# Attention decode with a squared-ReLU layer: the input is loaded twice, some matmuls change places, and two weight loads become one

## The chip, the cores and the metric

The kernel runs on one core of a Trainium2 chip. The metric is device time in microseconds (us) of one execution; the time of a kernel is the median of its runs.

## The reference, cut to what matters

Two tokens (B = 2) of width D = 512 go through one attention block with a long cache and one dense block, each after a layer norm and each with a residual:

```python
B, Sq, D = 2, 1, 512;  H, Sk, Dh = 32, 8192, 128;  F = 1792      # float32
q = (layernorm(x) @ wq) per head
p = softmax(q . k_cache * Dh ** -0.5)          # 64 pairs of head and token, 8192 keys each
h = x + (p . v_cache, heads side by side) @ wo
r = relu(layernorm(h) @ w1 + b1)
out = h + (r * r) @ w2 + b2
```

Each of the 64 pairs of head and token has 4 MB of keys and 4 MB of values, and each is read once. Nearly all of the 561 MB that the kernel reads is this cache.

## The kernel before, in words

**Storage.** One large SBUF tile, `ring`, has three places of 64 KB in each of 128 partitions. A place holds the keys and values of one pair. Place 2 first holds `wq` and, at the end, `wo`; place 0 holds `w1` and `w2` at the end.

**Beginning (lines 205 to 311).** The SP queue, which issues every load, issues `wq` into place 2, then the 2 rows of `x` into `xr` (line 210), then pairs 0 and 1 (line 212). A load is spread over 16 DMA engines, and each of them works off its share in the order in which it was issued; the 128 rows of 64 KB make eight packets for each engine. When `x` is there, DVE and ACT compute the layer norm of its two rows into `xnr` (lines 263 to 268). TensorE turns `xnr` into `xn` and `xr` into `hT` with four matmuls each against `ident`, multiplies `xn` with `wq` and turns the result into `QT`. When the last matmul that reads `wq` is over, SP issues pair 2 into place 2 (line 302).

**Loop (lines 321 to 365).** For 60 pairs, TensorE computes scores into one half of PSUM, DVE takes their maximum, ACT the exponentials, and DVE multiplies them with the values and adds up (four `scalar_tensor_tensor` of 2048 columns). SP issues the next pair into a place as soon as it is free.

**End (lines 470 to 598).** The last four pairs are written out one by one. `GROUPS` joins the partial results of the four quarters of the cache: group 0 has the heads 0 to 30, group 1 the last head. `wo` comes in as its first half, early, and then in pieces of 8, 6 and 2 heads (`WO_PIECES`); `w1` comes in three pieces and `w2` in five (`W2_PIECES`, blocks of 256 KB). `project` multiplies finished heads with `wo` into the PSUM bank `hp`. The last head's part goes another way: its effect on the normed input comes through `woc`, and its effect on the sum is added to the output bank `o`. `hidden` is the first dense layer (into `y`, bank 2 of `S[0]`). `y` is turned by DVE into `yT`; `a1` and `a2` are the bias and the squared ReLU. The second layer adds 14 blocks of four matmuls of 128 columns into `o`, which is copied to `res` and stored.

**Order and waits.** Outside the loop, instructions are recorded in a list (`Line.op`) in the written order, and `Line.plan` (line 68) finds the waits. Each tile's columns that an instruction reads or writes are remembered, with who wrote or read them; the rows (partitions) of a tile are not part of what is remembered:

```python
        return ap.tensor.name, lo, hi
```

An instruction waits for what touched the same columns before, if one of the two is a write, unless the same engine did it:

```python
                            if source == engine and (engine == "pe" or not w):
                                continue
                            needs[source] = max(needs.get(source, 0), n)
```

A load that SP issues is remembered as a source of its own, `("load", number)`, and not as `"sp"`. A wait stands in front of the waiting instruction in its engine's queue, and what is queued behind it waits as well. In addition, a load waits until the load eight before it has landed (`AHEAD`). The loads of pairs 0 to 2 in the beginning, lines 212 and 302, are given to SP by hand and carry no memory of what they write, save that line 302 waits for what reads place 2.

Of the kernel before, what the change touches and what calls it, by code (L numbers as in the profile page):

```python
# [4 lines left out]
AF = mybir.ActivationFunctionType  # L5
ALU = mybir.AluOpType
# [3 lines left out]
B, H, SK, DH, D, F = 2, 32, 8192, 128, 512, 1792  # L10
P = 128
NQ = 4
CS = SK // NQ
NH = DH // 32
DB = D // P
FB = F // P
FQ = F // NQ
BH = H * B
# [4 lines left out]
BLK = 512  # L23
GROUPS = [(0, 31), (31, 32)]
W1_PIECES = [2, 1, 1]
WO_PIECES = [8, 6, 2]
BIAS = 32
W2_PIECES = [4, 4, 3, 2, 1]
AHEAD = 8
# [141 lines left out]
def attention_block_kernel(nc, xd, kvd, wqd, wod, w1d, w2d, out):  # L171
    def sb(name, *shape):
        return nc.alloc_sbuf_tensor(name, [P, *shape], F32).ap()

    written = nc.alloc_semaphore("written")
    line = Line(nc)
# [8 lines left out]
    def place(u):  # L185
        return ring[:, u * ROW : (u + 1) * ROW]
# [11 lines left out]
    WO = place(2).rearrange("p (h c) -> p h c", h=H)  # L198
    b1T = ring[:, SLOTS * ROW : SLOTS * ROW + FB]
    b2T = ring[:, SLOTS * ROW + FB : SLOTS * ROW + FB + DB]  # L200
    W1 = place(0)[:, : DB * F].rearrange("p (d c) -> p d c", d=DB)
# [1 line left out]


    xr = sb("xr", D)
    xnr = sb("xnr", D)
    line.load(place(2), wqd)
    line.memset(xr, 0.0)
    line.memset(xnr, 0.0)
    line.load(xr[:B], xd)  # L210
    for i in range(2):
        line.op("sp", lambda e, i=i: e.dma_start(slot(i), kvd[i]).then_inc(kv_full[i], 16))
    line.op("sp", lambda e: e.sem_inc(s_free, 2))
# [4 lines left out]
    eps_t = sb("eps_t", 1)  # L218
# [3 lines left out]
    ident = sb("ident", P)  # L222
# [3 lines left out]
    quads = ident.rearrange("p (j m) -> p j m", j=NQ)  # L226
# [3 lines left out]
    def banks(k):  # L230
        return [S[k][:, n * BLK : (n + 1) * BLK] for n in range(NQ)]

    def clear(ap, n):
        line.act(ap, zero.to_broadcast([P, n]), AF.Copy)

    part = sb("part", B)
    xc = sb("xc", DB, B)
# [18 lines left out]
    bk = banks(1)  # L256
    clear(bk[0], BLK)
    clear(bk[1], BLK)
    xn = sb("xn", DB, B)
    hT = sb("hT", DB, B)  # L260
    xs = sb("xs", D)
    sx = sb("sx", 2)
    line.reduce(sx[:B, :1], xr[:B], ALU.add)
    line.fused(xnr[:B], sx[:B, :1].to_broadcast([B, D]), -1.0 / D, xr[:B], ALU.mult, ALU.add)
    line.fused(xs[:B], xnr[:B], 1.0, xnr[:B], ALU.mult, ALU.mult, accum_out=sx[:B, 1:])
    line.act(sx[:B, 1:], sx[:B, 1:], AF.Sqrt, bias=eps_t[:B], scale=1.0 / D)
    line.reciprocal(sx[:B, 1:], sx[:B, 1:])
    line.times(xnr[:B], xnr[:B], sx[:B, 1:])
    for t, (to, row) in enumerate(((xn, xnr), (hT, xr))):
        cols = bk[3][:, t * DB * B : (t + 1) * DB * B].rearrange("p (d b) -> p d b", b=B)  # L270
        for d in range(DB):
            line.matmul(cols[:, d, :], row[:, d * P : (d + 1) * P], ident[:, :B])
        line.copy(to, cols)
    warm = sb("warm", 1)
    line.act(warm, eps_t, AF.Exp)
    fold = sb("fold", 32)
# [3 lines left out]
    pick_all = sb("pick_all", P)  # L280
# [3 lines left out]
    for k in range(2):  # L284
        for d in range(DB):
            for j in range(NQ):
                n = k * NQ + j
                line.matmul(bk[k][32 * j : 32 * j + B, :], xn[:, d, :], WQ[:, d, n * BLK : (n + 1) * BLK],
                            start=(d == 0), stop=(d == DB - 1))
        line.act(big[:, k * BLK : (k + 1) * BLK], bk[k], AF.Copy)  # L290
    turned = bk[2][:, :BH].rearrange("p (k j m b) -> p k m j b", k=2, j=NQ, b=B)
    for k in range(2):
        for m in range(NQ):
            at = k * BLK + m * DH
# [11 lines left out]
    NM, LS, AC = ALL[:, :, 0], ALL[:, :, 1], ALL[:, :, 2:]  # L306
    OT = sb("OT", BH)
# [22 lines left out]
    with nc.Fori(0, LOOPED, SLOTS, engines=[ENGINE.PE, ENGINE.DVE, ENGINE.Activation],  # L330
                 head_slot={ENGINE.PE: 0, ENGINE.DVE: 128, ENGINE.Activation: 128}) as i0:
        for u in range(SLOTS):
            k = u % 2
            s, bk = S[k], banks(k)
# [6 lines left out]
            for n in range(CS // BLK):  # L341
                for j in range(NQ):
                    made = pe.matmul(bk[n][32 * j : 32 * j + 32, :], q3[:, u, :], keys(u)[:, j, n * BLK : (n + 1) * BLK],  # L343
                                     start=True, stop=True)
# [13 lines left out]
            for e in range(NH):  # L358
                v = values(u)[:, e]
                made = dve.scalar_tensor_tensor(v, v, 1.0, s, op0=ALU.mult, op1=ALU.mult,  # L360
                                                accum_out=st3[:, u, 2 + e : 3 + e])
# [12 lines left out]
    def maximum(i, k):  # L374
        line.reduce(NM[:, i : i + 1], S[k], ALU.max, negate=True)

    def exponentials(i, k):
        line.act(S[k], S[k], AF.Exp, bias=NM[:, i : i + 1], accum_out=LS[:, i : i + 1])

    def weighted(i, k, e, lo, hi, acc, by=1.0):  # L380

        v = values(i)[:, e, lo:hi]
        line.fused(v, v, by, S[k][:, lo:hi], ALU.mult, ALU.mult, accum_out=acc)

    def back(i, k, e):
        weighted(i, k, e, 0, CS, AC[:, i, e : e + 1])

    gm, w, lw, rl = (sb(n, BH) for n in ("gm", "w", "lw", "rl"))
# [6 lines left out]
    def weigh_max(n, pn):  # L395

        a, b = g_at[n]
        pn = pn[:, : NQ * (b - a)].rearrange("p (j i) -> p j i", j=NQ)
        for j in range(NQ):
            line.matmul(pn[:, j], pick[:, j, :], NM[:, a:b])  # L400

    def weigh_exp(n, pn):

        a, b = g_at[n]
        nb = b - a
        line.reduce(gm[:, :nb], pn[:, : NQ * nb].rearrange("p (j i) -> p i j", j=NQ), ALU.min)
        line.tensor(w[:, :nb], gm[:, :nb], NM[:, a:b], ALU.subtract)

    def weigh_rest(n, pl):

        a, b = g_at[n]
        nb = b - a
        line.tensor(lw[:, :nb], LS[:, a:b], w[:, :nb], ALU.mult)
        line.matmul(pl[:, :nb], pick_all, lw[:, :nb])
# [17 lines left out]
    def project(hs, hp):  # L432

        for h in hs:
            j = h % NQ
            line.matmul(hp[32 * j : 32 * j + B, :], OT[:, h * B : (h + 1) * B], WO[:, h, :],
                        start=(h < NQ), stop=(H - 1 - h <= NQ))

    def turn_rows(hp, ph):
        line.act(rows, hp, AF.Copy)  # L440
        ph = ph[:, : DB * B].rearrange("p (d b) -> p d b", b=B)
        for d in range(DB):
            line.matmul(ph[:, d, :], rows[:, d * P : (d + 1) * P], fold[:, :B])
        return ph
# [9 lines left out]
    def load_wo(a, b):  # L454

        cut = slice(a * D, b * D + (BIAS if b == H else 0))
        line.load(ring[:, 2 * ROW :][:, cut], wod[:, cut])
# [9 lines left out]
    bk0, bk1 = banks(0), banks(1)  # L467
# [29 lines left out]
    at = H // 2  # L497
    for n in WO_PIECES:
        load_wo(at, at + n)
# [14 lines left out]
    at = 0  # L514
# [3 lines left out]
    at = 0  # L518
# [4 lines left out]
    hp, sums, y, o = bk0  # L523
    y, o = y[:, :FQ], o[:, :P]
    clear(hp, D)
    clear(y, FQ)
    clear(o, P)
    maximum(last, 1)
    exponentials(last, 1)
    a, b = g_at[1]  # L530
    weigh_max(1, sums[:, :64])
    project(range(H // 2), hp)
    weigh_exp(1, sums[:, :64])
    line.act(w[:, :B], w[:, :B], AF.Exp)
    back(last, 1, 0)
    weigh_rest(1, sums[:, 64:128])
    line.act(warm, w[:, 0:1], AF.Sqrt)
    back(last, 1, 1)
    back(last, 1, 2)
    line.reciprocal(rl[:, :B], sums[:, 64 : 64 + B])  # L540
# [7 lines left out]

    line.times(aw2[:, 0, :NH], AC[:, last - 1, :], w[:, 0:1])
    line.times(aw2[:, 1, : NH - 1], AC[:, last, : NH - 1], w[:, 1:2])  # L550
    project(range(H // 2, H - 1), hp)
    ph = turn_rows(hp, sums[:, 192:256])
    weighted(last, 1, NH - 1, 0, CS // 2, aw2[:, 1, NH - 1 : NH], by=w[:, 1:2])
    weighted(last, 1, NH - 1, CS // 2, CS, aw2[:, 1, NH : NH + 1], by=w[:, 1:2])
# [2 lines left out]
    for e in range(NH + 1):  # L557
        at = 32 * min(e, NH - 1)
# [12 lines left out]
    def hidden(ds):  # L571
        for d in ds:
            for j in range(NQ):
                line.matmul(y[32 * j : 32 * j + B, :], xc[:, d, :], W1[:, d, j * FQ : (j + 1) * FQ],
                            start=(d == 0), stop=(d == DB - 1))
# [3 lines left out]
    line.matmul(var, ones_d, squares(xc))  # L579
    scale_of(var)  # L580
    hidden(range(2, DB))
    for j in range(NQ):
        line.matmul(o[32 * j : 32 * j + B, :], hT[:, j, :], ident, start=True, stop=False)
        line.matmul(o[32 * j : 32 * j + B, :], OT[:, a:b], WO[:, H - 1, j * P : (j + 1) * P], start=False, stop=False)
    yT = sb("yT", FB, 32)
    line.turn(yT.rearrange("p m r -> p (m r)"), y)
    a1 = sb("a1", FB, B)
# [4 lines left out]
    for m in range(FB):  # L592
        for j in range(NQ):
            line.matmul(o[32 * j : 32 * j + B, :], a2[:, m, :], W2[:, m, j * P : (j + 1) * P],
                        start=False, stop=(m == FB - 1))
    res = sb("res", P)
    line.copy(res, o)
    line.op("sp", lambda e: e.dma_start(out, res).then_inc(written, 16), [res], [])
# [35 lines left out]
```

## Time and profile before

| | us |
|---|---|
| median of 3 runs | 1303.70 |
| lowest and highest | 1303.56, 1303.97 |
| the profiled execution, whole | 1303.94 |
| its span, first to last instruction | 1302.6 |
| busy: DVE | 742.5 (57%) |
| busy: TensorE | 399.9 (31%) |
| busy: ACT | 143.9 (11%) |
| busy: DMA engines (16 together) | 99.7% of the span |
| read from HBM | 561.01 MB, 431 GB/s |

The 1.34 us between the span and the whole time lie before the first and after the last recorded instruction. PE is the TensorE matmul, DVE the VectorE, ACT the ScalarE, and SPq the queue of SyncE, which issues the transfers. A DMA's time to landing runs from its issue until its semaphore is complete.

### The profile page before, as it was taken

What the parts mean: (1) busy time and instruction counts of PE and PEld (TensorE: products, weight loads), DVE (VectorE), ACT (ScalarE), POOL (GpSimd) and SP (SyncE); (2) the same over time, 40 slices, a digit from 0 to 9 for tenths busy, and PEclk for the clock granted to TensorE, in tenths of its full rate; (3) what the DMA queues carried; (4) which work ended last, traced back from release to release, by engine and by line L of the source; (5) the groups of instructions that cost most, each with busy time, mean ns of one, the idle gap of its engine ahead of it and who ended that gap; (6) DMA issues with size and microseconds to landing.
All of it is one profiled execution on the core that took longest, in us unless ns stands there. A gap on an engine that the chain in (4) does not pass through costs nothing. (4 is left out here: it accounts for less than half of the span.)

```text
span 1302.6 us, 6694 instructions
## 1 busy us (share of the span) xinstructions
PE 399.9 (31%) x2424; PEld 109.8 (8%) x2424; DVE 742.5 (57%) x705; ACT 143.9 (11%) x149; POOL 0.7 (0%) x6
## 2 busy tenths in 40 slices
PE   1523223223313313322322322322322331331437
PEld 1100000000000000000000000000000000000113
DVE  1355665665665564665565565566566566557464
ACT  1011010011011011011011011101101101101111
POOL 0000000000000000000000000000000000000000
PEclk9676666667667667667667667666766756666657
DMA  9999999999999999999999999999999999999998
GB/s 419 420 445 425 443 427 441 427 439 431 433 437 421 447 423 445 425 445 425 443 425 439 431 435 435 425 443 423 445 425 445 425 443 425 441 429 437 420 429 363
DMA packets 11820, 561.19 MB, mean 431 GB/s; under 512 B 1314, under 2 KB 1442, under 8 KB 2468
## 3 DMA queue, kind: packets, MB, share of 16 engines
q1 hardware_dynamic: 11812, 561.08, 99.7%
q8 instruction: 5, 0.08, 0.0%
q14 instruction: 3, 0.02, 0.0%
HBM read 561.01 MB, written 0.07 MB: 431 GB/s over the span
## 5 line engine op out<-in xcount | busy, mean ns | idle before, releaser
L360 DVE SCALAR_TENSOR_TENSOR ring<-ring,s 128x2048 f32<-128x2048 f32 x240 | 534.7, 2283 | 136.2 <-DVEq L314 136.2
L343 PE MATMUL s<-ring,q 128*32 128x512 f32 x1920 | 333.0, 857 | 816.3 <-PEq L314 816.3
L349 DVE TENSOR_REDUCE st<-s 128x1 f32<-128x2048 f32 x60 | 137.5, 2292 | 325.3 <-DVEq L314 325.3
L355 ACT ACTIVATE s<-s,st 128x2048 f32<-128x2048 f32 x60 | 116.5, 1942 | 1031.7 <-ACTq L314 1031.7
L343 PEld LDWEIGHTS s<-ring,q 128*32 128x32 f32 x1920 | 84.5, 151 | 1064.0 <-issue 1064.0
L158 DVE SCALAR_TENSOR_TENSOR ring<-ring,s 128x2048 f32<-128x2048 f32 x15 | 33.6, 2283 | 6.6 <-ACT s L140 6.6
L136 PE MATMUL s<-ring,QR 128*32 128x512 f32 x128 | 24.3, 930 | 38.5 <-DMA ring<-in_kvd 24.9
L162 DVE TENSOR_REDUCE ALL<-s 128x1 f32<-128x2048 f32 x4 | 9.2, 2290 | 21.3 <-PE s L136 21.3
L360 DVE DVE_READ_ACCUMULATOR ring<-ring,s 128x1 f32 x240 | 19.8, 82 | 0.0
L364 DVE TENSOR_SCALAR ALL<-st 128x6 f32 x60 | 10.3, 171 | 15.1 <-DVEq L314 15.1
L140 ACT ACTIVATE s<-s,ALL 128x2048 f32<-128x2048 f32 x4 | 7.8, 1942 | 51.7 <-DVE ALL L162 51.7
L162 DVE TENSOR_REDUCE sx<-xr 2x1 f32<-2x512 f32 x1 | 0.7, 674 | 20.6 <-DMA xr<-in_xd 20.6
L355 ACT ACTIVATION_READ_ACCUMULATOR s<-s,st 128x1 f32 x60 | 11.6, 193 | 0.0
L136 PEld LDWEIGHTS s<-ring,QR 128*32 128x32 f32 x128 | 5.4, 162 | 56.3 <-DMA ring<-in_kvd 26.8
L136 PE MATMUL s<-ring,OT 128*2 128x512 f32 (+1 forms) x70 | 10.0, 701 | 0.0
L136 PE MATMUL s<-ident,xnr 128*128 128x2 f32 x8 | 1.9, 355 | 25.9 <-DVE xnr L154 25.9
L136 PE MATMUL s<-ring,xn 128*2 128x512 f32 x64 | 9.7, 773 | 0.0
L154 DVE TENSOR_SCALAR QT<-s 128x64 f32<-128x64 f32 x1 | 0.2, 224 | 10.6 <-PE s L136 10.6
L136 PE MATMUL s<-ring,a 128*2 128x128 f32 x112 | 4.8, 327 | 3.3 <-DMA ring<-in_w2d 2.2
L140 ACT ACT_TABLE_LOAD x4 | 5.1, 1283 | 0.8 <-PEq L627 0.7
L136 PE MATMUL s<-ALL,pick 128*128 128x62 f32 (+1 forms) x16 | 3.6, 369 | 4.8 <-DVE ALL L162 4.8
L351 DVE TENSOR_SCALAR q<-QT 128x96 f32 x20 | 4.9, 243 | 0.0
(84 smaller groups left out, 58.1 us busy)
## 6 DMA issues: line engine op xcount, KB each, us to landing
ring<-in_kvd SPq DMA_DIRECT2D x3, 4096.0 KB, 32.0
ring<-in_wod SPq DMA_DIRECT2D x1, 4096.0 KB, 28.6
ring<-in_kvd SPq DMA_DIRECT2D x1, 3072.0 KB, 28.1
ring<-in_wod SPq DMA_DIRECT2D x1, 2048.0 KB, 32.7
ring<-in_w2d SPq DMA_DIRECT2D x2, 1024.0 KB, 18.0
ring<-in_w1d SPq DMA_DIRECT2D x1, 1792.0 KB, 33.7
ring<-in_w1d SPq DMA_DIRECT2D x2, 896.0 KB, 23.6
ring<-in_wod SPq DMA_DIRECT2D x1, 1536.0 KB, 35.9
```

The lines of the kernel that those rows point to most:

```text
L136: self.op("pe", lambda e: e.matmul(out, lhsT, rhs, start=start, stop=stop), [lhsT, rhs], [out])
L140: self.op("act", lambda e: e.activation(out, in_, func, bias=bias, scale=scale, accum_out=accum_out), [in_, *more], [out] + ([] if accum_o ...
L154: self.op("dve", lambda e: e.tensor_scalar(out, in_, by, None, op0=ALU.mult), [in_, *more], [out])
L158: self.op("dve", lambda e: e.scalar_tensor_tensor(out, a, by, b, op0=op0, op1=op1, accum_out=accum_out), [a, b, *more], [out] + ([] if acc ...
L162: self.op("dve", lambda e: e.tensor_reduce(out, in_, axis=AX.X, op=op, negate=negate), [in_], [out])
L343: made = pe.matmul(bk[n][32 * j : 32 * j + 32, :], q3[:, u, :], keys(u)[:, j, n * BLK : (n + 1) * BLK], start=True, stop=True)
L349: dve.tensor_reduce(nm, s, axis=AX.X, op=ALU.max, negate=True).then_inc(m_full, 1)
L351: dve.tensor_scalar(q3, QT[:, bass.ds(i0 + SLOTS, SLOTS), None].to_broadcast([P, SLOTS, 32]), 1.0, None, op0=ALU.mult)
L355: act.activation(s, s, AF.Exp, bias=nm, scale=1.0, accum_out=ls).then_inc(e_full, 1)
L360: made = dve.scalar_tensor_tensor(v, v, 1.0, s, op0=ALU.mult, op1=ALU.mult, accum_out=st3[:, u, 2 + e : 3 + e])
L364: dve.tensor_scalar(ALL[:, bass.ds(i0 + u, 1)], st3[:, u : u + 1], 1.0, None, op0=ALU.mult).then_inc(kv_free, 1)
```

## The change

- `x` is loaded twice, by two loads in a row, into rows 0 to 1 and rows 32 to 33 of `xr`. The tile `xnr` and its clearing are dropped; the layer norm works in place on rows 32 to 33. One matmul per block of 128 columns now turns both pairs of rows, so four turns take the place of eight, with `hT` copied first and `xn` second.
- `WO_PIECES` is `[10, 6]` in place of `[8, 6, 2]`: one load fewer.
- Of the first 16 heads, seven are projected before the last pair's maximum is used, while DVE takes it, and nine after it. Of the other 15, the ten of the first piece come ahead of the matmul that sums the last head's `lw`, and five come later.
- The eight small matmuls that add `hT` and the last head to `o` move from ahead of the turn of `y` to behind the first four blocks of the second layer. In their old place stands one matmul of 512 columns whose result nobody reads.

```diff
-WO_PIECES = [8, 6, 2]
+WO_PIECES = [10, 6]
+EARLY = 7
...
-    xnr = sb("xnr", D)
     line.load(place(2), wqd)
     line.memset(xr, 0.0)
-    line.memset(xnr, 0.0)
-    line.load(xr[:B], xd)
+    for at in (0, 32):
+        line.load(xr[at : at + B], xd)
     for i in range(2):
         line.op("sp", lambda e, i=i: e.dma_start(slot(i), kvd[i]).then_inc(kv_full[i], 16))
...
+    xs = sb("xs", D)[32 : 32 + B]
+    sx = sb("sx", 2)[32 : 32 + B]
+    xnr = xr[32 : 32 + B]
...
-    for t, (to, row) in enumerate(((xn, xnr), (hT, xr))):
-        cols = bk[3][:, t * DB * B : (t + 1) * DB * B].rearrange("p (d b) -> p d b", b=B)
-        for d in range(DB):
-            line.matmul(cols[:, d, :], row[:, d * P : (d + 1) * P], ident[:, :B])
-        line.copy(to, cols)
+    cols = bk[3][:, : 2 * DB * B].rearrange("p (d t b) -> p d t b", t=2, b=B)
+    for d in range(DB):
+        line.matmul(cols[:, d], xr[:, d * P : (d + 1) * P], quads[:, :2, :B])
+    line.copy(hT, cols[:, :, 0])
+    line.copy(xn, cols[:, :, 1])
...
+    project(range(EARLY), hp)
     maximum(last, 1)
     exponentials(last, 1)
     a, b = g_at[1]
     weigh_max(1, sums[:, :64])
-    project(range(H // 2), hp)
+    project(range(EARLY, H // 2), hp)
...
-    weigh_rest(1, sums[:, 64:128])
+    line.tensor(lw[:, :B], LS[:, a:b], w[:, :B], ALU.mult)
     line.act(warm, w[:, 0:1], AF.Sqrt)
+    project(range(H // 2, H // 2 + WO_PIECES[0]), hp)
+    line.matmul(sums[:, 64 : 64 + B], pick_all, lw[:, :B])
...
-    project(range(H // 2, H - 1), hp)
+    project(range(H // 2 + WO_PIECES[0], H - 1), hp)
...
-    for j in range(NQ):
-        line.matmul(o[32 * j : 32 * j + B, :], hT[:, j, :], ident, start=True, stop=False)
-        line.matmul(o[32 * j : 32 * j + B, :], OT[:, a:b], WO[:, H - 1, j * P : (j + 1) * P], start=False, stop=False)
+    line.matmul(bk1[0][:B], xc[:, 0, :], W1[:, 0, :BLK])
...
-                        start=False, stop=(m == FB - 1))
+                        start=(m == 0), stop=(m == FB - 1))
+        if m == W2_PIECES[0] - 1:
+            for j in range(NQ):
+                at = o[32 * j : 32 * j + B, :]
+                line.matmul(at, hT[:, j, :], ident, start=False, stop=False)
+                line.matmul(at, OT[:, BH - B :], WO[:, H - 1, j * P : (j + 1) * P], start=False, stop=False)
```

More of the change, by code (lines that the diff above doesn't have):

```diff
@@ L260, in attention_block_kernel @@
     hT = sb("hT", DB, B)
[L261 to L268, printed above, removed]
-    for t, (to, row) in enumerate(((xn, xnr), (hT, xr))):
-        cols = bk[3][:, t * DB * B : (t + 1) * DB * B].rearrange("p (d b) -> p d b", b=B)
-        for d in range(DB):
-            line.matmul(cols[:, d, :], row[:, d * P : (d + 1) * P], ident[:, :B])
-        line.copy(to, cols)
+    xs = sb("xs", D)[32 : 32 + B]
+    sx = sb("sx", 2)[32 : 32 + B]
+    xnr = xr[32 : 32 + B]
+    line.reduce(sx[:, :1], xnr, ALU.add)
+    line.fused(xnr, sx[:, :1].to_broadcast([B, D]), -1.0 / D, xnr, ALU.mult, ALU.add)
+    line.fused(xs, xnr, 1.0, xnr, ALU.mult, ALU.mult, accum_out=sx[:, 1:])
+    line.act(sx[:, 1:], sx[:, 1:], AF.Sqrt, bias=eps_t[32 : 32 + B], scale=1.0 / D)
+    line.reciprocal(sx[:, 1:], sx[:, 1:])
+    line.times(xnr, xnr, sx[:, 1:])
+    cols = bk[3][:, : 2 * DB * B].rearrange("p (d t b) -> p d t b", t=2, b=B)
[3 more added lines that the diff above has]
+    line.copy(xn, cols[:, :, 1])
     warm = sb("warm", 1)
```

## The prediction

> **What bounds the kernel now.** I read the page first: its queue table says whether any engine matters at all.
>
> ```profile
> span 1302.6 us, 6694 instructions
> ...
> q1 hardware_dynamic: 11812, 561.08, 99.7%
> ```
>
> The one queue of loads keeps the 16 DMA engines busy for 99.7% of the span. So the kernel takes as long as 561 MB take, plus what lies before the first packet and after the last. An edit counts if it makes the engines stand idle, or if it shortens the two ends. The chain that ended last shows the back end:
>
> ```profile
> 1279.92 17.98 DMA ring<-in_w2d
> 1297.90 0.04 issue
> 1297.95 2.74 PE s L136 x48
> 1300.69 0.02 issue
> 1300.71 0.29 DVE res L147
> ```
>
> The last matmuls run 2.74 us without a pause, then comes the copy and the store. The front end is in the timeline (start, duration, engine, operation):
>
> ```profile
> 0.75 0.39 SPq L133 DMA_DIRECT2D ring<-in_wqd  x1
> 1.43 0.32 SPq L133 DMA_DIRECT2D xr<-in_xd  x1
> 1.80 0.94 SPq L212 DMA_DIRECT2D ring<-in_kvd  x2
> ...
> 22.66 0.67 DVE L162 TENSOR_REDUCE sx<-xr 2x1 f32<-2x512 f32 x1 [20.56 <-DMA xr<-in_xd]
> ```
>
> `x` is only 4 KB, but it lies behind the 8.4 MB of `wq` and lands at about 22.64. Pairs 0 and 1 are issued at 1.80, long before that. The table of stretches shows what this early issue buys (last column GB/s of the packets that start in the stretch, before it the summed packet time as a share of 16 engines):
>
> ```profile
> 1.50:1.75 0.25, 0.00 (x0) 0.00 (x0) 0.25 (x1) 0.25 (x1) 0.00 (x0) 1.00 0.00 0
> 1.75:2.00 0.25, 0.00 (x0) 0.00 (x0) 0.25 (x2) 0.25 (x1) 0.00 (x0) 1.00 8.76 2884
> 2.00:2.25 0.25, 0.00 (x0) 0.00 (x0) 0.10 (x3) 0.14 (x2) 0.00 (x0) 1.00 3.96 1311
> ...
> 21.50:21.75 0.25, 0.00 (x0) 0.00 (x0) 0.00 (x0) 0.00 (x0) 0.00 (x0) 1.00 1.21 524
> 21.75:22.00 0.25, 0.00 (x0) 0.00 (x0) 0.00 (x0) 0.00 (x0) 0.00 (x0) 1.00 2.45 1057
> 22.00:22.25 0.25, 0.00 (x0) 0.00 (x0) 0.00 (x0) 0.00 (x0) 0.00 (x0) 1.00 4.88 2105
> 22.25:22.50 0.25, 0.00 (x0) 0.00 (x0) 0.00 (x0) 0.00 (x0) 0.00 (x0) 1.00 1.21 524
> 24.00:25.00 1.00, 0.00 (x0) 0.00 (x0) 0.74 (x3) 0.19 (x1) 0.00 (x0) 1.00 2.42 1049
> ```
>
> A packet is 64 KB, so GB/s times the width counts packets. Eleven engines start their first packet between 1.75 and 2.00, five by 2.25. Those 16 packets take 8.76 x 0.25 + 3.96 x 0.25 = 3.18 us each. In the round at 24 they take 2.42. Between 21.5 and 22.5 the engines pass, one after the other (2, 4, 8, 2), from `wq` straight to pair 0, at 22.03 in the mean.
>
> **The second load of `x`: the one edit that touches the stream.** Both loads write the same columns of `xr`, in other rows. The planner remembers columns only, and a load is a source of its own, so the second load waits on SP until the first has landed. Behind it in SP's queue are pairs 0 and 1. They are now issued after `wq` has been read to the end, and all 16 engines run dry. The working:
> - The first load lands as before: 22.64. SP needs some 0.06 to go on (the second piece of `w1` is issued at 1262.71 behind a landing at 1262.65), so the second load of `x` is issued at 22.70. Pair 0 follows 0.37 later (1.43 to 1.80 before), at 23.07.
> - From issue to packets: `wq` was issued at 0.75 and its packets start at 1.95 in the mean (the middles of the two stretches, 11 and 5 engines): 1.20. So pair 0 starts at 24.27 in place of 22.03: **+2.24**. It can't be a gain, as there is nothing else to read. At its lowest the delay is 1.9: the store of the result has its first packets 0.84 after its issue.
> - The first packets into idle engines took 3.18, later ones 2.42. If pair 0 starts as `wq` did, that adds **+0.76**. The bounds are 0 (only the start of the execution is slow) and 0.76; I take 0.76, since this is the same kind of load, into as many idle engines, and no nearer row exists.
>
> The Trainium skill ("DMA: Bandwidth & Descriptors", Anatomy of one DMA) speaks against this edit too: a DMA has some 2 us of fixed cost, mostly the receipt of its last write, which only overlap hides. By that figure alone the price would be 2.0 in place of 3.0. The rows say more, since they hold the slower first packets as well.
>
> Nothing gives the delay back, as the loop is bound by the stream: pair 3 is issued at 64.56, when pair 2 is still coming in until some 82.
>
> **The rest of the beginning: nothing.** The second load lands at about 24.2 (the store, as small, took 1.5 from issue to landing), 1.55 later than `x` before. Four turns fewer give 1.87 back (eight instructions fewer at 27.98 for 1.87), and one clearing of 0.48 on DVE was never waited for. So the queries are ready at about 41.9 as before. Pair 2 is issued at 39.54, some 20 us before pair 1 is in: that is its cover, and pair 2 is due no earlier than before.
>
> **One load of `wo` fewer.** The bytes and their order stay. Between 1204 and 1297, with 18 smaller loads, the stretch moves 424 GB/s; the loop from 100 to 1200 moves 433. That is 2.1% of 93 us, 1.9 us in all and at most 0.11 for one load; part of it is instruction fetches. I take **-0.05**, between 0 and -0.11. Loads are issued as early as before or earlier, with 17 us and more from issue to landing, so none comes late.
>
> **Projections.** Seven heads go into 2.42 us in which TensorE waited for the last maximum. Two rounds of four, two passes each, take about 0.43 a pass at full clock: 1.7. At half clock they would push the joining by 1 us. Ten heads must now end before `lw` is summed: they may start when their piece lands, about 1276.1, and take 20 x 0.12 to 0.19 us, to 1279 or so; the sum was wanted at 1279.94. Five heads remain behind the last piece (1279.86) where fifteen ran until 1282.66, so `hT` comes some 0.8 earlier. None of it shows in the end: `hidden` waits for the last piece of `w1` at 1291.04. Without this cover, 0.8 would be a gain, and a late join a loss of up to 1. Price 0.
>
> **The matmuls in the second layer.** The eight small ones (1291.91 to 1292.54, 0.63 busy) lay beside the turn of `y` and cost nothing there. In their new place they fill the wait for the second piece of `w2`: the first four blocks end at 1294.72, plus 0.63 is 1295.35, and the piece lands at 1296.02. The unread matmul, two passes of 512 columns at 0.43 or 0.85 each, runs from 1292.1 to 1293.0 or 1293.8; the second layer begins at 1293.64. Cost 0, at most 0.2. What they can change is the clock. In these stretches of 3.41 us the second number is TensorE's busy time, and the third from the end its granted clock:
>
> ```profile
> 1267.45:1270.86 3.41, 1.18 (x12) 0.12 (x4) 2.15 (x1) 0.00 (x0) 0.00 (x0) 0.99 0.95 406
> 1270.86:1274.27 3.41, 3.22 (x16) 2.04 (x20) 1.42 (x4) 2.96 (x4) 0.00 (x0) 0.50 1.01 429
> ...
> 1291.34:1294.75 3.41, 2.25 (x56) 1.19 (x48) 1.31 (x4) 0.00 (x0) 0.00 (x0) 1.00 1.02 423
> 1294.75:1298.17 3.42, 1.28 (x40) 0.96 (x44) 0.00 (x0) 0.00 (x0) 0.00 (x0) 0.99 0.94 376
> 1298.17:1301.58 3.41, 2.47 (x48) 1.16 (x37) 0.29 (x1) 0.00 (x0) 0.00 (x0) 0.50 0.10 34
> ```
>
> After 1.18 and 1.28 busy the next stretch has half clock, after 2.25 full clock. The moved matmuls make the second to last one 1.28 + 0.63 = 1.91, nearer to 2.25. At full clock an instruction takes 1.05/32 = 0.033 us, at half 2.74/48 = 0.057. The last piece of `w2` lands at 1299.8, and its eight instructions then end at about 1300.1 in place of 1300.69: -0.55 at best. The Trainium skill ("TensorE: Matmul & The Clock Gate", Part 1) says that the window of 3.4 us runs freely, so that its position differs from run to run; one profile can't show that here. I take **-0.45**, between 0 and -0.55.
>
> **Sum.** From the profiled execution: 1303.94 + 2.24 + 0.76 - 0.05 - 0.45 = **1306.4**, which is 2.7 above the median of 1303.70 (the profiled execution was 0.24 above it). 0.2% of the time, about what a measurement of this kernel can tell from no change, is 2.6 us, up to 1306.3; the forecast lies just beyond it.
>
> **Rivals.**
> - *The engines restart at full pace* (not slower by 0.2%). Place: the first round of pair 0. Price: the 0.76 falls away, 1305.7; with first packets 0.84 after the issue 1305.3. It decides as soon as first packets take under about 3.05. For it: the slow packets are seen only at the very start of the execution. Against it: nothing in the profile shows idle engines that start a load quickly. Chance 0.31. The Trainium skill's fixed 2 us, named above, belongs to this rival (1303.94 + 2.0 - 0.05 - 0.45 = 1305.4).
> - *The end runs at half clock.* The moved matmuls then end at 1293.67 + 48 x 0.057 = 1296.4, past the landing at 1296.02, and the remaining 80 instructions end 4.57 later, at 1301.0, 0.3 later than before: 1303.94 + 2.95 + 0.3 = 1307.2. Against it: TensorE has more work than before in the windows that decide. Chance 0.08.
> - *The change doesn't do what I read*: pairs 0 and 1 get out before `x` lands, or are hidden. Then only the end moves: 1303.94 - 0.5 = 1303.4. The order of SP's queue speaks against it. Chance 0.04.
>
> **How the numbers follow.** The forecast has 0.57, of which 0.50 is over 0.2% slower and 0.07 (the end fully gained) is not; its own range is 1306.0 to 1306.9. The restart adds 0.02 to slower and 0.29 to the same, the half clock 0.08 to slower, the last rival 0.03 to the same and 0.01 to faster. Together: slower 0.60, same 0.39, faster 0.01. The range reaches from the restart rival (1305.1) to the half clock (1307.3).
>
> **What would show it.** Right: SP issues the second `x` at 22.7 and pair 0 at 23.1; no 64 KB packet starts between 22.5 and 24.0; the first round then lasts about 3.2; the loop is the same, 3 us later. Wrong: pair 0 issued before 22, a first round of 2.4 us, or a last piece of `w2` that lands at other than 1302.1 to 1303.

## The result and the profile after

The changed kernel takes 1306.27 us (median of 17 runs, 1305.88 to 1307.4), the kernel before 1303.82 (17 runs, 1303.51 to 1304.9): 2.45 us or 0.19% slower, ratio 1.002 with the 95% interval [1.0012, 1.0027]. The forecast was 1306.4. The profiled execution of the changed kernel took 1305.97, near the lowest of its runs, and the one of before 1303.94, above its median; so the two profiles differ by 2.03 and the medians by 2.45.

The page of the changed kernel, its first line and its queue table:

```profile
span 1304.6 us, 6680 instructions
...
q1 hardware_dynamic: 11672, 561.08, 99.6%
```

The bytes are the same but for the 4 KB of the second load, and the queue of loads is still what binds. SP's queue (start, duration, engine, operation):

```profile
0.75 0.39 SPq L134 DMA_DIRECT2D ring<-in_wqd  x1
1.43 21.27 SPq L134 DMA_DIRECT2D xr<-in_xd  x2
22.75 0.83 SPq L212 DMA_DIRECT2D ring<-in_kvd  x2
38.63 0.33 SPq L303 DMA_DIRECT2D ring<-in_kvd  x1
```

The two loads of `x` are merged into one row that reaches from 1.43 to 22.70: the second, whose issue takes 0.24 us, starts at 22.46, behind the landing of the first. Pairs 0 and 1 are issued at 22.75 in place of 1.80. SP's waits name it:

```profile
SPq L134 <- DMA xr<-in_xd: 20.7, 1, 20.7
```

What the DMA engines do meanwhile, in stretches (last column GB/s of the packets that start in it, before it the DMA share):

```profile
22.25:22.50 0.25, 0.00 (x0) 0.00 (x0) 0.00 (x0) 0.00 (x0) 0.00 (x0) 1.00 0.00 0
22.50:23.25 0.75, 0.00 (x0) 0.00 (x0) 0.00 (x0) 0.00 (x0) 0.00 (x0) 1.00 0.00 0
23.25:23.50 0.25, 0.00 (x0) 0.00 (x0) 0.00 (x0) 0.00 (x0) 0.00 (x0) 1.00 0.04 16
23.50:23.75 0.25, 0.00 (x0) 0.00 (x0) 0.00 (x0) 0.00 (x0) 0.00 (x0) 1.00 2.35 786
23.75:24.00 0.25, 0.00 (x0) 0.00 (x0) 0.16 (x1) 0.00 (x0) 0.00 (x0) 1.00 8.56 2884
24.00:24.25 0.25, 0.00 (x0) 0.00 (x0) 0.25 (x1) 0.00 (x0) 0.00 (x0) 1.00 0.76 262
24.25:24.50 0.25, 0.00 (x0) 0.00 (x0) 0.25 (x1) 0.00 (x0) 0.00 (x0) 1.00 0.68 262
...
26.50:27.50 1.00, 0.46 (x3) 0.46 (x3) 0.48 (x1) 1.00 (x1) 0.00 (x0) 1.00 2.42 1049
```

Where 16 packets had followed `wq` at once, nothing but the 4 KB of `x` starts before 23.50. Pair 0's first packets then start 3, 11, 1 and 1 to a stretch, at 23.88 in the mean, in place of 22.03: +1.85. Their shares times 0.25 add up to 3.09 us, against 2.42 in the round behind them: +0.67. The end of the chain:

```profile
1283.63 17.97 DMA ring<-in_w2d
1301.60 0.04 issue
1301.64 0.62 PE s L137 x16
1302.26 0.01 issue
1302.28 0.44 PE s L137 x8
1302.72 0.02 issue
1302.74 0.29 DVE res L148
```

TensorE now keeps up: where 48 instructions ran without a pause after the third piece, it waits for each of the last two. The last piece lands at 1302.23 (before 1299.77, +2.46), and the copy begins 0.51 later (before 0.94). +2.46 and -0.43 give the 2.03 by which the copy is later (1302.74 against 1300.71). Granted clock in TensorE's last stretches, third from the end; its busy time is the second number:

```profile
1293.39:1296.80 3.41, 2.71 (x34) 0.71 (x30) 1.48 (x5) 0.06 (x1) 0.00 (x0) 1.00 1.02 422
1296.80:1300.21 3.41, 2.19 (x76) 1.54 (x64) 0.00 (x0) 0.00 (x0) 0.00 (x0) 1.00 0.97 391
1300.21:1303.62 3.41, 1.86 (x48) 0.96 (x48) 0.29 (x1) 0.00 (x0) 0.00 (x0) 1.00 0.14 52
```

The end runs at full clock. Whether the moved matmuls did that is a question for the experiments.

### The profile page after: what moved, and what is told of

It is laid out like the page before. It is cut to its first block, busy times and chain, and to the rows that moved or that the text cites. A ratio compares the mean times of both kernels' runs of the same rounds, so it can differ in the third digit from the quotient of the medians.

```text
span 1304.6 us, 6680 instructions
## 1 busy us (share of the span) xinstructions
PE 410.0 (31%) x2418; PEld 110.0 (8%) x2418; DVE 742.2 (57%) x704; ACT 143.8 (11%) x149; POOL 0.7 (0%) x6
## 5 line engine op out<-in xcount | busy, mean ns | idle before, releaser
L344 PE MATMUL s<-ring,q 128*32 128x512 f32 x1920 | 345.5, 885 | 807.0 <-PEq L315 807.0
L137 PE MATMUL s<-ring,xc 128*2 128x448 f32 (+1 forms) x34 | 5.8, 747 | 0.3 <-DVE xc L151 0.3
```

Source lines behind the costliest of these rows:

```text
L137: self.op("pe", lambda e: e.matmul(out, lhsT, rhs, start=start, stop=stop), [lhsT, rhs], [out])
```

## The experiments

The theory: the wait of the second load keeps pairs 0 and 1 back, the engines stand idle for 1.85 and start 0.67 slower, and this is the whole loss. The main rival: the loss comes from the other edits, and the loop's cover takes up the delay.

| kernel | median, us | before beside it | difference | ratio, 95% interval |
|---|---|---|---|---|
| one load, DVE copies the rows (e1) | 1303.52 | 1303.65 | -0.13 | 0.9998 [0.9989, 1.0007] |
| before, second load only (e2) | 1306.36 | 1303.65 | +2.71 | 1.002 [1.0011, 1.0029] |
| before, end only (e3) | 1303.52 | 1303.65 | -0.13 | 1.0001 [0.9992, 1.001] |
| three loads in a chain (e4) | 1307.45 | 1303.65 | +3.80 | 1.003 [1.0018, 1.0042] |
| second load from ACT (e5) | 1303.58 | 1303.70 | -0.12 | 0.9997 [0.9988, 1.0007] |
| before, `wo` and projections only (e6) | 1303.80 | 1303.70 | +0.10 | 1.0 [0.9991, 1.0009] |
| e1 and one more unread matmul (e7) | 1303.74 | 1303.70 | +0.04 | 0.9999 [0.999, 1.0008] |
| pair 0 in two loads (e8), one run | 1305.87 | 1303.70 | +2.17 | |

**e1: the change without the wait.**

```diff
-    for at in (0, 32):
-        line.load(xr[at : at + B], xd)
+    line.load(xr[:B], xd)
...
+    line.copy(xnr, xr[:B])
     line.reduce(sx[:, :1], xnr, ALU.add)
```

> The changed kernel with one load of x; DVE copies its rows into rows 32 to 33 (0.5 us off the path), so no load waits on SP. All else of the change stays. Theory (the second load idles the engines): pairs 0 and 1 are issued at 1.8 again, packets of pair 0 follow those of wq without a gap, and the time falls by 2.3 to 2.6 against the changed kernel, to 0.1 to 0.5 below the kernel before. Rival (the loss comes from the fewer loads of wo, the projections or the moved matmuls): it stays 2 us or more above the kernel before. Rival (the delay at the start is made up for by the loop's cover): no change against the changed kernel.

Measured 1303.52. The stretches have the packets of pair 0 between 21.5 and 22.5 again, and a first round of 2.42:

```profile
21.50:22.50 1.00, 0.00 (x0) 0.00 (x0) 0.02 (x1) 0.00 (x0) 0.00 (x0) 1.00 2.44 1053
22.50:24.00 1.50, 0.00 (x0) 0.00 (x0) 1.43 (x3) 0.00 (x0) 0.00 (x0) 1.00 0.00 0
24.00:25.00 1.00, 0.00 (x0) 0.00 (x0) 0.97 (x3) 0.00 (x0) 0.00 (x0) 1.00 2.42 1049
```

The whole loss goes with the second load, so both rivals fall. Against the kernel before the result is as expected; against the changed kernel it is 2.75 lower, more than the 2.3 to 2.6 expected. The two ran at different times; with each taken against the kernel before that ran beside it, the distance is 2.45 + 0.13 = 2.58.

**e2: the wait without the rest of the change.**

```diff
-    line.load(xr[:B], xd)
+    for at in (0, 32):
+        line.load(xr[at : at + B], xd)
```

> The kernel before, with x loaded a second time into rows 32 to 33 of xr, which only adds the wait (in the transposes of xr these rows meet zeros of the identity). Theory: the stream's end comes 2.5 later as in the changed kernel, and without the gain at the end the whole time is 2.4 to 2.7 above the kernel before (1.85 of idle engines and 0.67 of slow first packets). Rival (the loss is elsewhere): within 0.3 of the kernel before.

Measured +2.71, a hair above the 2.4 to 2.7 expected. The first round is 2.47 x 1.25 = 3.09 us, the same as in the changed kernel:

```profile
22.25:23.25 1.00, 0.00 (x0) 0.00 (x0) 0.00 (x0) 0.00 (x0) 0.00 (x0) 1.00 0.00 0
23.25:23.75 0.50, 0.00 (x0) 0.00 (x0) 0.00 (x0) 0.00 (x0) 0.00 (x0) 1.00 0.02 8
23.75:25.00 1.25, 0.00 (x0) 0.00 (x0) 1.14 (x2) 0.00 (x0) 0.00 (x0) 1.00 2.47 839
```

So the load alone makes the loss. Its profile holds a surprise at the other end, which e6 repeats: here the order of the second layer is that of before, and still the end runs at full clock.

**e3: the end alone.** The last two hunks of the change, put into the kernel before.

```diff
-    for j in range(NQ):
-        line.matmul(o[32 * j : 32 * j + B, :], hT[:, j, :], ident, start=True, stop=False)
...
+    line.matmul(bk1[0][:B], xc[:, 0, :], W1[:, 0, :BLK])
...
+        if m == W2_PIECES[0] - 1:
+            for j in range(NQ):
...
```

> The kernel before, with only the moved small matmuls and the unread one. Theory: the last piece of w2 lands as before, TensorE has full clock behind it, and the kernel is 0.1 to 0.5 faster than before; in the profile 0.5 from landing to copy in place of 0.94. Rival (they cost time on the path, the gain seen in the changed kernel's profile comes from another position of the clock's windows): 0 to 0.3 slower.

Measured -0.13 in the median, and the interval includes a ratio of 1. In its profile the last piece lands at 1299.78 and the copy begins at 1300.29, 0.51 later, as expected. But that 0.51 is not proof, as e2 and e6 show it, within 0.01, with the old order. The third from the end in these stretches of e6 is the clock:

```profile
1294.48:1297.89 3.41, 1.60 (x52) 0.98 (x44) 0.00 (x0) 0.00 (x0) 0.00 (x0) 1.00 0.96 385
1297.89:1301.30 3.41, 1.83 (x48) 0.95 (x48) 0.29 (x1) 0.00 (x0) 0.00 (x0) 1.00 0.13 46
```

Here the stretch ahead of the last one begins 0.27 earlier than in the profile of before and holds 1.60 of TensorE's work in place of 1.28, without any edit to that work. Its busy time alone doesn't decide, though. The profile of before has, a little earlier, a stretch with 2.70 that is followed by one at half clock:

```profile
1284.51:1287.93 3.42, 2.70 (x32) 1.70 (x36) 1.12 (x8) 0.00 (x0) 0.00 (x0) 0.99 0.99 413
1287.93:1291.34 3.41, 3.41 (x22) 0.72 (x18) 0.17 (x1) 0.26 (x1) 0.00 (x0) 0.51 1.02 422
```

So the rule that the prediction reads from three stretches (half clock after 1.18 and 1.28, full clock after 2.25) doesn't hold for all of them, and what the clock goes by stays open. Of the three profiles with the old order (before, e2, e6) one has the end at half clock, of the seven with the new order none. That the moved matmuls raise the odds of full clock is not shown; what they are worth in the median is some 0.1 and is lost in the spread of the runs.

**e4: a third load in the chain.**

```diff
-    for at in (0, 32):
+    for at in (0, 64, 32):
```

> The changed kernel with a third load of x (rows 64 to 65, which the identity's zeros leave out) ahead of the second: one more wait in the chain. Theory (idle time is paid per load in the chain, the slow first round of 64 KB packets once): each load costs issue to landing, 1.4 (22.45 to 23.82 for the second one), so 1.3 to 1.5 above the changed kernel, 3.7 to 4.0 above the kernel before. Rival (every stop costs the whole 2.45): 4.9 above the kernel before. Rival (the cost is one of the second load's own rows, not of waiting): nothing added.

Measured 3.80 above the kernel before, within 3.7 to 4.0: the third load adds 1.18 to the changed kernel's median (1.09 to e2's, which ran beside it) and not another 2.45. Against the changed kernel that is less than the 1.3 to 1.5 expected. Pair 0 is issued at 24.12, 1.37 later than in the changed kernel, and its first round takes 2.33 x 1.25 = 2.91 in place of 3.09, 0.18 less; the two together make 1.19. The price is one latency for each load of the chain, and one slow start.

```profile
22.50:25.00 2.50, 0.00 (x0) 0.00 (x0) 0.00 (x0) 0.00 (x0) 0.00 (x0) 1.00 0.02 3
25.00:26.25 1.25, 0.00 (x0) 0.00 (x0) 0.89 (x2) 0.00 (x0) 0.00 (x0) 1.00 2.33 839
```

**e5: the same wait in another queue.**

```diff
-    for at in (0, 32):
-        line.load(xr[at : at + B], xd)
+    line.load(xr[:B], xd)
+    line.load(xr[32 : 32 + B], xd, engine="act")
```

> The changed kernel with its second load of x issued from ACT's queue in place of SP's. The wait on the first load stays, but pairs 0 and 1 are no longer queued behind it. Theory (the cost is that SP stands still): pairs 0 and 1 are issued at 1.8, no gap, and the time is that of the kernel with one load, within 0.3 of the kernel before; the second load of x lands some microseconds later than 23.8, which the cover of the queries hides. Rival (a small load that is issued late waits in the DMA engines behind all that is queued, whoever issues it): x lands only when pairs 0 and 1 are in, at about 62, the queries are ready at about 80, pair 2 is issued at 78 and the engines stand idle for some 17 us: about 1320.

Measured 1303.58: no loss. The timeline shows that the wait is still there, on ACT, and that the late load is slow:

```profile
22.71 0.54 ACTq L134 DMA_DIRECT2D xr<-in_xd  x1
...
30.00 0.68 DVE L163 TENSOR_REDUCE sx<-xr 2x1 f32<-2x512 f32 x1 [28.43 <-DMA xr<-in_xd]
```

The 4 KB are used 7.3 us after their issue, and not behind pairs 0 and 1 as the rival had it. They start among the 64 KB packets of pair 0, some 4 us after the issue: this stretch of the DMA engines moves 16 packets of 64 KB (1049 KB) and 4 KB more.

```profile
26.50:27.50 1.00, 0.00 (x0) 0.00 (x0) 0.00 (x0) 0.49 (x1) 0.00 (x0) 1.00 2.44 1053
```

Pair 2 is issued at 44.76 in place of 39.54, which its cover of 20 us takes up. It is not the wait that costs, but what is queued behind it.

**e6: the load of `wo` and the projections.** Put into the kernel before:

```diff
-WO_PIECES = [8, 6, 2]
+WO_PIECES = [10, 6]
+EARLY = 7
...
+    project(range(EARLY), hp)
...
-    project(range(H // 2), hp)
+    project(range(EARLY, H // 2), hp)
...
+    project(range(H // 2, H // 2 + WO_PIECES[0]), hp)
...
```

> The kernel before with only the merged load of wo and the projections split at the last maxima. Theory (hidden behind the last piece of w1; one load fewer is worth 0 to 0.1): within 0.15 of the kernel before; hT some 0.8 earlier against the landing of the last half piece of the values. Rival (the larger piece keeps TensorE and the sum waiting): 0.3 or more slower.

Measured +0.10, within 0.15; no load came late. The turned rows are there when DVE ends the last half of the values (1283.63), where before `hT` waited 0.83 for TensorE; as forecast, nothing of it reaches the end.

**e7: one more unread matmul.** In e1, behind the eighth block of the second layer:

```diff
+        if m == W2_PIECES[0] + W2_PIECES[1] - 1:
+            line.matmul(bk1[0][:B, :256], xc[:, 0, :], W1[:, 0, :256])
```

> The changed kernel with one load of x (DVE copies the rows) and one more unread matmul of 256 columns behind the second piece of w2, where TensorE waits for the third. Theory (the moved matmuls already make most ends run at full clock): at the same time as without it, 0 to 0.1 lower, 0.1 to 0.3 below the kernel before in the median. Rival (the end still falls to half clock in many executions): 0.2 to 0.4 below the kernel with one load.

Measured 1303.74, 0.22 above e1, which ran beside other runs of the kernel before (+0.04 against -0.13). Both numbers miss what was expected, 0 to 0.1 below e1 and 0.1 to 0.3 below the kernel before, and the rival misses as well. The matmul brings nothing that can be told from no change. No version tried beats the kernel before by more than its runs scatter.

**e8: smaller first packets.** Pair 0 as two loads, keys first, then values, each with its own semaphore.

```diff
+    keys_full = nc.alloc_semaphore("keys_full")
+    line.op("sp", lambda e: e.dma_start(slot(0)[:, :HALF], kvd[0][:, :HALF]).then_inc(keys_full, 16))
+    line.op("sp", lambda e: e.dma_start(slot(0)[:, HALF:], kvd[0][:, HALF:]).then_inc(kv_full[0], 16))
+    line.op("sp", lambda e: e.dma_start(slot(1), kvd[1]).then_inc(kv_full[1], 16))
...
+    line.op("pe", lambda e: e.wait_ge(keys_full, 16))
```

> The changed kernel with pair 0 issued as two loads, keys and values, so that the first packets into the idle engines are of 32 KB in place of 64. It measures the slow first round. Theory (a fixed start-up of about 0.67 us for the first packet): the first 32 KB packets take 1.21 + 0.67 = 1.9 us, the following 1.21. Rival (a lower rate while all engines start in step, 64 KB in 3.09): the first takes 1.54 and the second too. The whole time stays within 0.4 of the changed kernel's.

```profile
23.50:24.50 1.00, 0.00 (x0) 0.00 (x0) 0.68 (x1) 0.00 (x0) 0.00 (x0) 1.00 1.80 524
...
25.25:26.10 0.85, 0.00 (x0) 0.00 (x0) 0.67 (x2) 0.15 (x1) 0.00 (x0) 1.00 1.42 617
```

The 16 first packets of 32 KB take 1.80 each, the next 16 take 1.42 x 0.85 = 1.21. The surcharge is 0.59 on half the bytes, against 0.67 on 64 KB, and the second packet has none. So it is paid at the start, nearly independent of the size, and not as a lower rate over the whole packet.

It isn't a fixed price of each engine's first packet, however. In e4 the first packets of pair 0 begin spread over almost 1 us, and those that begin late pay less:

```profile
25.00:25.50 0.50, 0.00 (x0) 0.00 (x0) 0.17 (x1) 0.00 (x0) 0.00 (x0) 1.00 3.86 1311
25.50:26.25 0.75, 0.00 (x0) 0.00 (x0) 0.71 (x2) 0.00 (x0) 0.00 (x0) 1.00 1.31 524
```

The ten packets that begin before 25.50 take 3.86 x 0.50 x 16 / 10 = 3.09 each, the six behind them 1.31 x 0.75 x 16 / 6 = 2.62: 0.67 and 0.20 more than 2.42. A short slow phase after the stop, shared by all engines, would fit this and e8; what makes it is open. The whole time of e8, 1305.87, stays within 0.4 of the changed kernel's.

## Why the prediction was right, and where its terms were off

- **The wait and its place.** Right, and shown from three sides: taken away (e1), made alone (e2), moved to another queue (e5).
- **Idle engines, +2.24.** Measured +1.85. The term was mis-sized, as each of its steps was a little long. The second load of `x` was issued at 22.46 and not at 22.70, as the first had landed earlier: in the profiles with one load it is first used between 22.39 (e3) and 22.66 (before), so the row taken was the latest of them. Pair 0 followed 0.29 later in place of 0.37, and its packets 1.13 after that in place of 1.20. The sum of these is 0.39. The measured 1.85 lies a hair below the 1.9 that the text gives as the lowest, and for another reason: the packets did not come 0.84 after the issue, the steps ahead of it were shorter.
- **Slow first round, +0.76.** Measured +0.67. The row taken for it, the first load of the execution, was the right one, and the rival that sees it only there falls: e2, e4 and e8 show it 24 to 26 us into the execution. The 2 us of fixed cost that the Trainium skill gives ("DMA: Bandwidth & Descriptors", Anatomy of one DMA) would have been short by 0.5 of the measured 2.46. That section measures loads that GpSimd issues, and these were issued by SP: here the 4 KB load into idle engines took 1.4 from its issue to its use, and the measurement decides. That 2 us came so near is chance, as they hold no slow first round.
- **One load fewer, -0.05.** The stream came to +2.46 where idle time and first round give 2.52, and in e2, with no load fewer, to +2.84 (last landing at 1302.61); e6 alone shows +0.10 in the median. Too small to be told.
- **Projections, the beginning, the moved matmuls' own time: 0.** Right. The scaled queries were done at 40.70 (before 41.61), the sum of `lw` was done in time, the small matmuls ended at 1297.94 and the next piece landed at 1298.48. The second load took 1.4 from its issue to its use in place of the 1.5 of the store, which with its 64 KB is not as small as the text says.
- **The clock at the end, -0.45.** Between the two profiles it is -0.43, as forecast. That was also the most there is to gain: the last eight matmuls took 0.44 at full clock and not the 8 x 0.033 = 0.26 behind the -0.55. Its cause, more work in the stretch ahead, is not shown (e3). For the median the term says little: it was taken against an execution whose end ran at half clock, while e2 and e6 show the old order at full clock too. e1 against before gives -0.13 for everything but the load. That the windows' position differs from execution to execution, as the Trainium skill says ("TensorE: Matmul & The Clock Gate", Part 1), these profiles bear out: the last change to full clock came at 1291.34 in the profile of before and at 1291.06 in that of e6, with TensorE's order at the end the same.
- **The total.** Of 3.0 for the stream, 2.5 came. Against the profiled execution of the changed kernel (1305.97) the sum of 1306.44 is 0.47 too high, all of it from the stream. The median lies 0.30 above that execution, for no reason that the runs show, and so 1306.4 against 1306.27 looks better than the terms deserve; that much is luck. 2.45 is 0.19%, a little under the 2.6 that the text called distinguishable: the larger chance (0.60) was on a loss over 0.2%, and the measured one sits within 0.2% by a hair, though its interval (0.12% to 0.27%) holds both and does not reach down to zero.

## What to carry to other kernels

Where a stream of loads is the bound, ask of each new load not how many bytes it has but what is queued behind its wait: 4 KB cost 2.5 us here, because a tracker that knows columns and no rows took two loads into different rows for a conflict. Put a load that must wait into a queue with nothing urgent behind it, or let an idle engine make the copy. And a gain that hangs on a free-running clock is read from several executions: two profiles showed 0.43 where the medians show 0.1.

## What the runs showed of the hardware

- The first packets into idle DMA engines take 0.6 to 0.7 longer, for 64 KB as for 32 KB, and again each time that the engines have stood idle (3.18 at the start of the execution, 3.09 at 24). Packets that begin half a microsecond behind the first of them pay less: 0.20 in the chain of three, whose round takes 2.91 in the mean.
- A 4 KB load that is issued from another queue while the engines work on 64 KB packets took 7.3 us from its issue until it was used; into idle engines it took 1.4 (issued at 22.46, used at 23.84).
- The stretches of 3.41 us between which TensorE's clock changes lie elsewhere in each execution (a border at 1294.75 in the profile of before, at 1294.48 in that of e6). A stretch with 1.60 us of busy time was followed by full clock, and one with 2.70 by half clock, so the busy time alone doesn't tell the next clock.
